# A long convolution with its spectra kept on the chip: three blocks of 192 channels, data as the stationary operand

## The chip, the core and the metric

The kernel runs on one core of a Trainium2 chip. The core has a matrix engine (TensorE; PE in the profile, its weight loads PEld), a vector engine (VectorE, DVE), an activation engine (ScalarE, ACT), a general engine (GpSimd, POOL) and a queue engine (SyncE, SP) that issues nearly all DMA transfers. The engines run side by side, each strictly in the order of its own instructions, and wait for one another by semaphores. Matmuls read the on-chip memory SBUF and write the accumulators in PSUM; ACT or DVE must copy ("evacuate") what stands there back to SBUF.

The metric is the device time of one execution, in microseconds; lower is better. The profiled execution has a span from the first instruction to the last. The engines' busy times and the waits are those of this one execution.

## The reference: what is computed

Two independent parts with 2048 positions and 576 channels each, concatenated. Part A is attention in which each position looks at 8 positions, 2 apart; part B multiplies a long causal convolution (2048 taps for each channel) with q.

```python
def _A_ref(x, wqkv, wo):                 # H = 32 heads of 18, W, dil = 8, 2
    qkv = (x @ wqkv).reshape(B, S, 3, H, Dh).transpose(2, 0, 3, 1, 4)
    q, k, v = qkv[0], qkv[1], qkv[2]
    idx = pos[:, None] - (jnp.arange(W) * dil)[None, :]
    ...
    logits = jnp.einsum("bhsd,bhswd->bhsw", q, kg) * scale
    attn = softmax(where(mask, logits, -1e9))
    o = jnp.einsum("bhsw,bhswd->bhsd", attn, vg)
    return o.transpose(0, 2, 1, 3).reshape(B, S, D) @ wo

def _B_ref(q, k, v, shift_k, ssm_k, ssm_D):
    k_shift = sum(k_pad[:, t:t + S, :] * shift_k[:, ks - 1 - t] for t in range(4))
    kv = k_shift * v
    y_f = rfft(pad(kv, S)) * rfft(pad(ssm_k, S))     # length 4096
    y = irfft(y_f)[:, :S].astype(bfloat16)
    return q * (y + kv * ssm_D)

return jnp.concatenate([_A_ref(...), _B_ref(...)], axis=-1)
```

## The kernel before, in words

The work of both parts is cut into small steps. A long string, `ORDER`, lists them one by one; a table, `STEP`, gives the function for each short name, and the program is emitted in exactly this order. So the order in the string is the order on each engine and on the SP queue. A letter behind a step chooses one of two PSUM pools (`a`, `b`; two buffers of two banks each) and the engine of the evacuation (`s` ACT, `v` DVE; mostly ACT by default, in `evac`, L101 and L103).

Part A: x is loaded and transposed by DMA (`xt`, L357); `qk` and `qt` project it to q and k (L362, L390), `v` to v (L369). For each of the 8 offsets `lm` multiplies q with the shifted k on DVE (L478, L482) and `lb` sums over each head's channels by matmuls (L487, L495). `sm` is softmax in two halves of the positions. `pm` multiplies the weights with the shifted v on DVE (L577), `ps` sums over the 8 offsets (L587, 64 x 64 tiles with the identity), `po` multiplies by wo (L599) and stores.

Part B is a long convolution by a two-level Fourier transform: position = 16 a + b, with 128 values of a in the partitions and 16 of b. `cv` makes the short convolution and kv on DVE, in four chunks of four b (L448, L451, L453). `kt` transposes the filter (L466). `sx` and `kp` are the first level for kv and for the filter: a matmul by a 128-point table `T1` (L419), 128 frequencies in the partitions. A second level has to mix the 16 values of b, so its data must stand differently over the partitions. The kernel does that turn through DRAM: each `sx`/`kp` stores its spectrum to the scratch tensors Dx and Dk (L426), `xl`/`kl` load them turned (L536), `xs`/`ks` are the second level (`s2`, L530, table `W2`), for eight groups of frequencies and channels. `gp` multiplies the two spectra on DVE (L552), all four products of real and imaginary parts, `gi` is the inverse second level (L565, tables `IAt`) and stores to the scratch Dy; `yl` loads it turned (L610), `ys` is the inverse first level (L623) and multiplies with q (L627). `ql` loads q. The tables come from iotas, a bitwise wrap on DVE and a sine on ACT (`t2`, `t3`, `tw`, `ia`).

All large buffers lie in ten areas of SBUF; several buffers with lives one after the other share an area.

Of the kernel before, what the change touches and what calls it, by code (L numbers as in the profile page):

```python
# [10 lines left out]
ALU = mybir.AluOpType  # L11
# [7 lines left out]
tj ld wm.11:b tv t2 xt.3.0 xt.3.1 sk:b lwq.0.0 t3 lwt xt.3.3 xt.3.2 tw xt.3.4 lwq.1.1 qk.0.0.3:a t1 t0 lwq.0.1 lk.0  # L19
cv.0.0 cv.0.1 xt.2.4 lv.0 qk.1.1.3:a t4 cv.0.2 xt.2.0 wt:v cv.0.3 xt.2.2 qk.0.1.3:av xt.2.3 cv.0.4 ia:b qt.3:a xt.2.1  # L20
cv.0.5 lk.1 qk.1.1.2:b lkn.0 lkn.1 cv.0.6 lwq.1.0 lkn.3 cv.0.7 qt.2:b cv.1.1 cv.1.0 qk.0.1.2:a lkn.4 cv.1.2 cv.1.3
cv.1.4 sx.0.0:a lkn.2 xt.1.4 xt.1.0 xt.1.1 xt.1.2 sx.1.0:b qk.1.0.3:b xt.1.3 sx.0.1:a sx.0.2:a cv.1.5 kt.5:bs lk.2
qk.1.0.2:b sx.1.1:a kt.0:a sx.1.2:bv cv.1.6 qk.0.1.1:b kp.0.0:a kp.0.1:bv cv.2.1 qt.1:a xt.0.1 lv.1 kp.0.2:b cv.2.0
qk.0.0.1:a kp.5.0:av xt.0.0 kt.1:b kp.5.1:b xt.0.3 kp.5.2:av xt.0.2 cv.1.7 qk.0.0.2:a kp.1.0:bv t5 kp.1.1:b kt.4:a
xt.0.4 cv.2.2 kp.1.2:a kt.3:bs cv.2.3 cv.2.4 sx.2.0:b qk.1.0.1:a cv.2.5 lk.3 cv.2.6 cv.3.1 sx.2.1:b sx.2.2:b sx.3.0:a
lv.2 qk.0.1.0:a sx.3.1:b sx.3.2:b qk.1.1.1:a cv.3.0 kp.3.0:b kp.3.1:a qt.0:b cv.3.2 lv.3 kp.3.2:a cv.3.3 cv.3.4
qk.0.0.0:b cv.3.5 kp.4.0:b kp.4.1:a kp.4.2:a lwv kt.7:bs qk.1.0.0:b cv.2.7 cv.3.6 kt.2:a cv.3.7 kp.7.0:a kp.7.1:b
kp.7.2:b kt.6:as sx.4.0:b qk.1.1.0:a lm.6.2 lm.0.2 lm.0.0 sx.4.1:b sx.4.2:b v.0:a lm.0.1 sx.6.0:b lm.6.1 sx.6.1:b
lb.0:a sx.6.2:b sx.7.0:a lm.6.0 sx.7.1:b v.2:a sx.7.2:b lb.6:a sx.5.0:b lm.1.0 sx.5.1:a lm.1.1 sx.5.2:b lm.7.0 v.3:a
lb.1:a xl.2 vz kp.2.0:a kp.6.0:b kp.2.1:a lm.7.1 v.8:b lm.4.2 v.5:a xl.3 lm.2.0 lb.7:a lm.2.2 kp.6.1:b kp.2.2:b lm.2.1  # L30
kp.6.2:a v.6:a lb.2:b lm.4.0 v.1:a v.7:b lm.4.1 kl.2 lb.4:b vh.0 lm.3.0 lm.3.1 lm.5.0 v.4:a lb.3:a xs.2.0:b xs.2.1:a
kl.3 lm.5.1 ks.2.0:b lb.5:a vh.1 gp.2.0 vh.2 sm.0.0 sm.1.0 ks.3.0:b xl.0 sm.0.1 ks.2.1:b lwo.3 kl.0 xs.3.0:a ql.0
ks.3.1:b gp.2.1 xs.0.0:a sm.0.2 xs.3.1:b gp.3.0 sm.0.3 gi.3.0:av sm.0.4 gp.3.1 ks.0.0:a xl.1 sm.0.5 sm.1.1 ks.0.1:b
sm.0.6 kl.1 xl.5 xs.0.1:a sm.1.2 gi.3.1:b sm.0.7 gp.0.0 sm.0.8 sm.1.3 ks.1.0:b xs.1.0:a gi.0.0:b kl.5 ql.3 sm.0.10
gp.1.0 ks.1.1:a gp.0.1 lwo.0 pm.0.3 gi.2.0:b xs.1.1:a ks.5.0:b xl.6 kl.6 sm.1.4 gi.0.1:a gi.2.1:b pm.0.1 pm.0.0
ps.0.3:a gp.1.1 ps.0.1:a xs.5.0:a xs.5.1:b pm.0.5 xs.6.0:a gp.5.0 pm.0.4 ks.5.1:b kl.4 ps.0.0:a pm.0.8 sm.1.5 ks.6.0:b
gi.1.0:a ps.0.5:b xl.4 gp.5.1 xs.6.1:a xl.7 gi.1.1:b sm.1.6 ks.6.1:a pm.0.2 gi.5.0:b ps.0.8:a kl.7 gi.5.1:b xs.4.0:a
ks.4.0:b ks.4.1:a ps.0.4:b sm.1.7 yl.1 ql.1 gp.6.0 xs.4.1:a gp.6.1 gp.4.0 lwo.2 gi.6.0:b ps.0.2:a gi.4.0:a lwo.1
pm.0.7 gp.4.1 gi.6.1:b pm.0.6 sm.1.8 ys.1.0:as sm.1.10 yl.3 xs.7.0:b gi.4.1:a xs.7.1:b ks.7.0:a ps.0.7:b ql.5 gp.7.0
ps.0.6:b ks.7.1:a pm.1.1 ys.1.1:bs po.0.0.0 po.0.1.0 yl.0 pm.1.8 gp.7.1 ql.7 ps.1.1:a pm.1.0 yl.2 pm.1.6 gi.7.0:b  # L40
gi.7.1:a ps.1.8:b ys.3.0:as ys.3.1:bs ps.1.0:a ps.1.6:a pm.1.5 ql.2 ys.0.0:bs ys.0.1:bs yl.7 po.0.1.1 pm.1.2 pm.1.4
ps.1.5:b ys.2.0:as yl.5 ys.2.1:a ps.1.2:b pm.1.7 pm.1.3 ps.1.4:a yl.6 po.0.0.1 yl.4 ps.1.7:a ys.7.0:b ys.7.1:as
ps.1.3:av ys.5.0:b ys.5.1:a po.1.0.1 ql.6 ql.4 po.1.0.0 po.1.1.0:v ys.6.0:bs ys.6.1:as ys.4.0:as ys.4.1:bs po.1.1.1
# [4 lines left out]
def kernel(  # L48
# [21 lines left out]
    HD = D // 2  # L70
    PS = bass.MemoryType.PSUM
# [11 lines left out]
    dram = ctx.enter_context(tc.tile_pool(name="dram", bufs=1, space=bass.MemoryType.DRAM))  # L83
# [67 lines left out]
    class Ring:  # L151
# [18 lines left out]
    row0 = const.tile([128, 128], BF16, name="row0")  # L170
    T1 = const.tile([128, 2, 128], BF16, name="T1")
    IB = const.tile([128, 2, 128], BF16, name="IB")
    W2 = const.tile([128, 2, 32, 4, 16], BF16, name="W2")
    IAt = const.tile([128, 3, 16, 128], BF16, name="IAt")
    Eh = const.tile([128, HC + 2, H], BF16, name="Eh")
    maskb = const.tile([128, 32], BF16, name="maskb")
    Db = const.tile([128, D], BF16, name="Db")

    r1, r2, r3, r4, r5, r6, r7, r8, r9, r10 = (
        Area(f"area{i}", n) for i, n in enumerate((18560, 16384, 5 * S, 4 * D, 5 * 2 * D, 19 * D, 28 * D, 2 * S, 5 * D + S + 640, 4 * D)))  # L180
    xns = [(r4 if i < 1 else r2).take(4, D) for i in range(4)]
# [494 lines left out]
```

## Time and profile before

| | us |
|---|---|
| runs | 215.08, 218.06, 219.16; median 218.06 |
| span of the profiled execution | 219.4 |
| DMA moved in it | 50.78 MB, of which HBM read 28.83 MB and written 18.87 MB |
| mean granted TensorE clock | 0.953 |

The table of groups shows for each line and operation the number of instructions, their busy time, the mean in ns and the idle time of the engine just before, with what ended it. The page's DMA part, in transfers, size of one and time from issue to landing:

```profile
Dx<-area SPq DMA_DIRECT2D x16, 288.0 KB, 3.2
Dk<-area SPq DMA_DIRECT2D x16, 288.0 KB, 3.6
...
area<-Dk SPq DMA_DIRECT2D x8, 576.0 KB, 5.5
Dy<-area SPq DMA_DIRECT2D x8, 576.0 KB, 4.0
area<-Dy SPq DMA_DIRECT2D x8, 576.0 KB, 6.1
```

### The profile page before, as it was taken

To read this page: it belongs to the slowest core of one execution; us is meant where nothing else is said; L and a number is where in the kernel's file an instruction comes from. 1 tells how busy PE (TensorE), PEld (TensorE's weight loads), DVE (VectorE), ACT (ScalarE), POOL (GpSimd) and SP (SyncE) were. 2 spreads that over 40 slices of the span, in tenths; PEclk is the share of its full clock that TensorE was granted. 3 is DMA by queue.
4 is the path that set the end of the run, shared out by engine and by line. 5 is a ranking of instruction groups with operands and counts; after the bars stand their busy time and mean duration, and the time that the engine had idled before them with its cause. 6 is when DMAs were issued, how large, how long until landed. Compare 5 with 4: busy or idle time off the path is not lost.

```text
span 219.4 us, 6207 instructions
## 1 busy us (share of the span) xinstructions
PE 193.8 (88%) x2663; PEld 120.3 (55%) x2663; DVE 185.4 (85%) x165; ACT 161.4 (74%) x243; POOL 7.4 (3%) x30
## 2 busy tenths in 40 slices
PE   7696899999899999999998588689995999999890
PEld 2133445556345545566754355556663697777670
DVE  7759996699879999999998899999997399998150
ACT  2627649676699979867479999999995959544442
POOL 7500000000000000000000000000000000000000
PEclk9769599999999999999999969999998899999999
DMA  4799994999997873574769939977999946989984
GB/s 94 150 316 281 371 157 96 279 276 175 226 336 236 225 219 110 184 230 141 209 129 243 352 130 305 288 241 258 341 243 194 348 131 170 355 242 323 266 246 140
DMA packets 60187, 50.78 MB, mean 231 GB/s; under 512 B 14624, under 2 KB 54112, under 8 KB 60160
## 3 DMA queue, kind: packets, MB, share of 16 engines
q1 hardware_dynamic: 60110, 50.24, 82.4%
q8 instruction: 20, 0.33, 0.6%
q0 software_dynamic: 48, 0.15, 0.4%
q14 instruction: 7, 0.06, 0.1%
q10 hardware_dynamic: 2, 0.00, 0.0%
HBM read 28.83 MB, written 18.87 MB: 217 GB/s over the span
## 4 chain that ended last, share of the span: by engine, by line
PE 50%; ACT 15%; DMA 12%; DVE 8%; issue 7%; SPq 6%; ACTq 1%; DVEq 0%
ACT area L101 11%; PE psA L362 8%; PE psA L369 7%; PE psB L362 6%; DMA area<-Dy 4%; PE psA L599 4%; SPq L357 4%; DVE area L577 3%; PE psB L419 3%; DMA out_dram<-area 3%; PE psA L419 2%; DMA area<-in_A_wqkv_dram 2%; PE psB L565 2%; PE psB L369 2%; PE psA L495 2%
## 5 line engine op out<-in xcount | busy, mean ns | idle before, releaser
L101 ACT ACTIVATE area<-psA 128x576 bf16<-128x576 f32 (+5 forms) x112 | 79.3, 745 | 35.2 <-PE psB L599 10.1
L101 ACT ACTIVATE area<-psB 128x576 bf16<-128x576 f32 (+6 forms) x118 | 82.1, 743 | 12.4 <-PE psB L362 4.3
L577 DVE TENSOR_TENSOR area<-area,area 128x4096 bf16<-128x4096 bf16 x18 | 40.6, 2283 | 0.0
L478 DVE TENSOR_TENSOR area<-area 128x4096 bf16<-128x4096 bf16 x16 | 35.6, 2283 | 0.3 <-PE psB L495 0.3
L362 PEld LDWEIGHTS <-area 128*128 128x128 bf16 x160 | 16.5, 104 | 24.6 <-issue 8.2
L362 PE MATMUL psA<-area,area 128*128 128x512 bf16 x100 | 26.0, 411 | 1.9 <-DMA area<-in_A_x_dram 0.9
L448 DVE TENSOR_TENSOR area<-area,area 128x2304 bf16<-128x2304 bf16 x16 | 21.4, 1355 | 5.1 <-DMA area<-in_B_k_dram 4.8
L552 DVE TENSOR_TENSOR area<-area 128x2304 bf16<-128x2304 bf16 x16 | 21.5, 1352 | 4.7 <-ACT area L101 4.7
L530 PEld LDWEIGHTS <-W 128*64 128x64 bf16 x256 | 14.4, 111 | 15.5 <-issue 12.2
L599 PE MATMUL psB<-area,area 32*128 32x288 bf16 x288 | 18.7, 281 | 0.8 <-issue 0.8
L599 PE MATMUL psA<-area,area 32*128 32x288 bf16 x288 | 19.1, 281 | 0.2 <-DVE area L627 0.2
L599 PEld LDWEIGHTS <-area 32*128 32x128 bf16 x576 | 15.9, 93 | 4.0 <-issue 2.7
L587 PEld LDWEIGHTS <-ident 64*64 64x64 bf16 x576 | 15.0, 106 | 5.5 <-issue 3.7
L369 PEld LDWEIGHTS <-area 128*32 128x32 bf16 x360 | 14.1, 141 | 6.5 <-issue 1.3
L369 PE MATMUL psA<-area,area 128*32 128x512 bf16 x280 | 16.6, 382 | 0.5 <-DMA area<-in_A_wqkv_dram 0.5
L565 PEld LDWEIGHTS <-IAt 64*128 64x128 bf16 x256 | 13.1, 99 | 7.0 <-issue 2.7
L530 PE MATMUL psA<-area,W 128*64 128x288 bf16 x136 | 13.1, 292 | 3.9 <-ACT area L101 1.9
L451 DVE TENSOR_TENSOR area<-area,area 128x2304 bf16<-128x2304 bf16 x12 | 16.3, 1354 | 0.2
L362 PE MATMUL psB<-area,area 128*128 128x512 bf16 x60 | 15.3, 405 | 0.0
L530 PE MATMUL psB<-area,W 128*64 128x288 bf16 x120 | 12.8, 310 | 2.0 <-ACT area L101 0.6
L419 PE MATMUL psB<-area,T 128*128 128x384 bf16 x58 | 13.3, 327 | 0.9 <-ACT area L101 0.9
L419 PEld LDWEIGHTS <-T 128*128 128x128 bf16 x96 | 8.8, 98 | 9.7 <-issue 3.7
(107 smaller groups left out, 201.2 us busy)
## 6 DMA issues: line engine op xcount, KB each, us to landing
Dx<-area SPq DMA_DIRECT2D x16, 288.0 KB, 3.2
Dk<-area SPq DMA_DIRECT2D x16, 288.0 KB, 3.6
area<-Dx SPq DMA_DIRECT2D x8, 576.0 KB, 5.1
area<-Dk SPq DMA_DIRECT2D x8, 576.0 KB, 5.5
Dy<-area SPq DMA_DIRECT2D x8, 576.0 KB, 4.0
area<-Dy SPq DMA_DIRECT2D x8, 576.0 KB, 6.1
area<-in_A_wo_dram SPq DMA_DIRECT2D x4, 648.0 KB, 11.5
area<-in_B_k_dram SPq DMA_DIRECT2D x4, 576.0 KB, 5.0
```

The source lines that it names most:

```text
L101: nc.scalar.activation(dst, src, ACT.Copy, **({} if scale is None else {"scale": scale}))
L362: nc.tensor.matmul(ps[:, u, :], w[:, kb, cols[u]:cols[u] + 128], xT[:, kb, t], start=(kb == 0), stop=(kb == 4))
L369: nc.tensor.matmul(ps[32 * a:32 * a + 32, u, :], wv[:, kb, 2 * n + u:D:DH], xT[:, kb, 512 * a:512 * a + 512], start=(kb == 0), stop=(kb == ...
L419: nc.tensor.matmul(ps[:, ri, 0:384], T1[:, ri, :], sf[:, 384 * ch:384 * ch + 384], start=True, stop=not extra)
L448: nc.vector.tensor_tensor(tB if k else tAr[c], kfull[:, 4 * c + 3 - j:4 * c + 7 - j, :], skb[:, j, :].unsqueeze(1).to_broadcast([128, 4, D ...
L451: nc.vector.tensor_tensor(tAr[c], tAr[c], tB, ALU.add)
L478: nc.vector.tensor_tensor(prr.get((n, h)), q2[h], k2[h][:, :, o0:o0 + S], ALU.mult)
L530: nc.tensor.matmul(ps[64 * hp:64 * hp + 64, im, 0:HD], W2[:, im, 8 * g + 2 * prl + hp].rearrange("p l f -> p (l f)"), Wt[:, 2 * prl + hp, ...
L552: nc.vector.tensor_tensor(Pv, Xv.unsqueeze(2).to_broadcast([128, 2, 2, 2 * HD]), Kv.unsqueeze(1).to_broadcast([128, 2, 2, 2 * HD]), ALU.mult)
L565: nc.tensor.matmul(ps[:, hp, 0:HD], IAt[r, tab, 4 * g + 2 * hv + u, :], Pp[(i, hv)][r, n, u, :], start=(n == 0), stop=(n == 3), tile_posit ...
L577: nc.vector.tensor_tensor(Pr.get((hv, p)), vv, Lt[:, :, 256 * hv:256 * hv + 256].unsqueeze(2).to_broadcast([128, W, 2, 256]), ALU.mult)
L599: nc.tensor.matmul(pss[e][:, b, 0:HD], Os[hv][g, d // 2, r, 128 * (d % 2):128 * (d % 2) + 128], wo4[g, d, d0:d1], start=(d == 0), stop=(d ...
```

## The change

The three scratch tensors go, and with them `xl`, `kl`, `yl` and every store into them. The channels are taken in three blocks of 192 (`BD`), each in 48 groups of four channels (`G`).

The first level now holds the data as the stationary operand and streams the table: for each group, a weight of 128 positions a x 64 columns (16 b, 4 channels) and the 128 columns of `T1`, once for the real part and once for the imaginary part, side by side in the two column halves of the array (`first`; steps `sx`, `kp`). The result has (part, b, channel) in the partitions, so that the second level can follow at once: for each of the 128 frequencies one matmul with a table of its own (`E2`) over the 96 columns of kv's and the filter's groups (`second`, steps `s2`). Its result `XKS` holds the spectra of kv and of the filter; `sw` puts a copy of the filter's with its two halves of 64 partitions exchanged beside them by two DMA transfers, `gp` makes two products for each frequency in place (three instructions a block), `gi` is the inverse second level with the products as the stationary operand and the table `F2` as the moving one, and `ys` the inverse first level with one table for each b (`T2`). There is one buffer each for the first level (`A`), the spectra (`XKS`) and the inverse (`B`, over the first third of `XKS`). The D term is added to the filter's tap 0 on POOL (`add_D`) and no longer by a matmul.

The convolution runs over 16 b x 192 channels at a time (3072 elements a partition). The tables: `t3` on POOL, `tc` wrap and sine, `tw` four scalings into `E2`, `tf` for `F2`, `ty` eight steps for `T2`, `tp` small helpers.

Part A changes where the memory map does: x is transposed by DMA twice, quarter by quarter for q and k (`xt`) and again for v (`xv`); the products' buffers for `lm` lie over wq, the last quarters of x and the convolution's buffers; `ps` works in 32 x 32 tiles on four pairs of channels at a time, so that five groups of 128 rows of the attention output come out, and `po` multiplies them as whole arrays, with wo loaded in that arrangement. `ORDER` is rewritten throughout.

```diff
-    dram = ctx.enter_context(tc.tile_pool(name="dram", bufs=1, space=bass.MemoryType.DRAM))
-    Dk = dram.tile([2, 32, 128, HD], BF16, name="Dk")
-    Dx = dram.tile([2, 32, 128, HD], BF16, name="Dx")
-    Dy = dram.tile([2, 32, 128, HD], BF16, name="Dy")
...
+    rA, rX, rQ, rC, rD, rL, rY = (Area(f"area{i}", n) for i, n in enumerate((12288, 18432, 18528, 14464, 13120, 4096, 3072)))
+    A = rA.take(128, 2, G)
...
+    XKS = rX.take(3, G, 128)
+    rX.reset()
+    B = rX.take(2, NT, BD)
...
+    wq = rC.take(5, 2 * D)
+    xqs[1] = rC.take(5, 512)
+    tA, tB = rC.take(NT, BD), rC.take(NT, BD)
+    xqs[0] = xqs[1]
+    rC.reset()
+    prr = Ring(*[rC.take(2, S) for _ in range(3)])
+    phr = Ring(rC.take(2, 2, 512))
...
+    kfs += [rD.take(NT + 3, BD)] * 2
+    kvs += [rD.take(NT, BD)] * 2
...
+    def add_D(q):
+        kn = knr[q]
+        nc.gpsimd.tensor_tensor(kn[0:96, 0:1], kn[0:96, 0:1], Dc[0:96, q:q + 1], ALU.add)
...
+    def t_second():
+        nc.gpsimd.iota(g2, pattern=[[4, 128], [512, 16]], base=0, channel_multiplier=0)
+        nc.gpsimd.tensor_scalar(n2[:, :, 0, :], g2, sc_f[:, 5:6], sc_f[:, 6:7], op0=ALU.mult, op1=ALU.add)
+        nc.gpsimd.tensor_scalar(n2[:, :, 1, :], n2[:, :, 0, :], 2048.0, None, op0=ALU.add)
+
+    def t_wrap(k):
+        r = slice(64 * k, 64 * k + 64)
+        nc.vector.tensor_single_scalar(n2[:, r], n2[:, r], 8191, ALU.bitwise_and)
+        nc.scalar.activation(C2[:, r], n2[:, r], ACT.Sin, bias=pib[:], scale=-2.0 * np.pi / 8192)
+
+    def t_e2(k):
+        nc.vector.tensor_scalar(E2[:].rearrange("p f (r d g) -> p (f r) d g", r=2, d=4)[:, :, k, :],
+                                C2.rearrange("p f r g -> p (f r) g"), dm_e[:, k:k + 1], None, op0=ALU.mult)
...
+    def t_t2(k):
+        nc.gpsimd.iota(tb, pattern=[[1, 2], [16, 128]], base=2 * k, channel_multiplier=0)
+        for ri in range(2):
+            nc.gpsimd.tensor_scalar(tn[:, :, ri, :], tb, sc_f[:, 10:11], 2048.0 * (1 + ri), op0=ALU.mult, op1=ALU.add)
+        nc.vector.tensor_single_scalar(tn, tn, 8191, ALU.bitwise_and)
+        nc.scalar.activation(T2[:, 2 * k:2 * k + 2], tn, ACT.Sin, bias=pib[:], scale=-2.0 * np.pi / 8192)
...
+            nc.vector.tensor_tensor(kvo[e].rearrange("p g b d -> p b g d"), tA.rearrange("p b (g d) -> p b g d", d=4),
+                                    kvs[e].rearrange("p b (g d) -> p b g d", d=4), ALU.mult)
...
+    def first(src, key, e, j):
+        ps = psb()
+        for g in range(8):
+            lhs = src[:, 8 * j + g].rearrange("p b d -> p (b d)")
+            for ri in range(2):
+                nc.tensor.matmul(ps[64 * ri:64 * ri + 64, g // 4, 128 * (g % 4):128 * (g % 4) + 128], lhs, T1[:, ri, :],
+                                 start=True, stop=True, tile_position=(0, 64 * ri))
+        evac(A[:, :, key, 8 * j:8 * j + 8], ps[:].rearrange("p a (g f) -> p f (a g)", g=4))
+
+    def second(e, j):
+        ps = psb()
+        for u in range(8):
+            f = 8 * j + u
+            nc.tensor.matmul(ps[:, u // 4, 128 * (u % 4):128 * (u % 4) + 2 * G], E2[:, f, :], A[:, f].rearrange("p k g -> p (k g)"),
+                             start=True, stop=True)
+        evac(XKS[:, 0:2, :, 8 * j:8 * j + 8].rearrange("p k g f -> p (k g) f"),
+             ps[:].rearrange("p a (u n) -> p n (a u)", u=4)[:, 0:2 * G, :])
+
+    def swap_k(e, r):
+        o = 64 * r
+        nc.sync.dma_start(XKS[o:o + 64, 2], XKS[64 - o:128 - o, 1])
+
+    def g_prod(e, c):
+        g = slice(16 * c, 16 * c + 16)
+        P = XKS[:, 1:3, g, :].rearrange("p t g f -> p t (g f)")
+        nc.vector.tensor_tensor(P, P, XKS[:, 0, g, :].rearrange("p g f -> p (g f)").unsqueeze(1).to_broadcast([128, 2, 2048]), ALU.mult)
+
+    def g_inv(e, j):
+        ps = psb()
+        for g in range(8):
+            for t in range(2):
+                nc.tensor.matmul(ps[:, g // 4, 128 * (g % 4):128 * (g % 4) + 128], XKS[:, 1 + t, 8 * j + g, :], F2[:, t, :],
+                                 start=(t == 0), stop=(t == 1))
+        evac(B.rearrange("p r b (g d) -> p (r b) g d", d=4)[:, :, 8 * j:8 * j + 8, :],
+             ps[:].rearrange("p a (g r d) -> p r (a g) d", g=4, d=4))
...
+        for v in range(4):
+            for ri in range(2):
+                nc.tensor.matmul(ps[:, v // 2, BD * (v % 2):BD * (v % 2) + BD], T2[:, 4 * j + v, ri, :], B[:, ri, 4 * j + v, :],
+                                 start=(ri == 0), stop=(ri == 1))
...
+        for n in range(W):
+            for c in range(m):
+                P = Pr[(hv, 4 * g + c)] if g < 2 else Pr[(hv, 8)]
+                for a in range(4):
+                    r = slice(32 * a, 32 * a + 32)
+                    nc.tensor.matmul(pss[a // 2][32 * c:32 * c + 32, a % 2, 0:w], ident[r, r],
...
+        for di, (d0, d1) in enumerate(DCH):
+            for g in range(5):
+                nc.tensor.matmul(ps[:, di, 0:HD], Os[hv][:, g, a, 128 * u:128 * u + 128], wo5[:, g, d0:d1],
+                                 start=(g == 0), stop=(g == 4))
```

The part of the new order from the second level of block 0 to the first `lm`, and the end of the order:

```
s2.0.12:bv s2.0.8:a cv.1.6 kt.1.1:bs qk.0.1.1:b qk.1.1.1:a qt.1:a lk.2 cv.1.7 sx.1.5:b kp.1.5:b sx.1.1:a sw.0.0 sw.0.1
qk.0.0.1:a cv.2.0 lv.2 cv.2.1 kp.1.3:b t5 cv.2.2 lkn.5 sx.1.2:b kp.1.0:a qk.1.0.1:a xt.0.2 sx.1.0:b kp.1.4:b gp.0.1
xt.0.4 sx.1.4:a gp.0.0 gp.0.2 gi.0.3:a xt.0.1 gi.0.0:bv gi.0.1:b gi.0.4:av cv.2.3 gi.0.5:a cv.2.4 gi.0.2:b sx.1.3:a
cv.2.5 xt.0.0 cv.2.6 xt.0.3 cv.2.7 kp.1.1:b xv.0.2 qt.0:a qk.1.1.0:bv qk.0.0.0:a lm.0.2 qk.1.0.0:a ql.0 qk.0.1.0:b
...
po.0.2.1:a pm.1.5 pm.1.4 pm.1.6 pm.1.8 po.0.1.1:b po.0.3.1:b ys.2.2:a ys.2.1:a ps.1.1:b ps.1.2:av po.1.1.0:b
po.1.2.0:bv po.1.3.0:av po.1.3.1:b po.1.1.1:bv po.1.2.1:av po.1.0.0:av po.1.0.1:a
```

495 lines of the change are left out of this document (205 added, 290 removed).

## The prediction, made before the changed kernel was run

> **What bounds the kernel now.** I read the busy times of the profile page first, then the busy time of each engine by stage, then the instructions by form, then the chain of waits and the list of who waits for whom.
>
> ```profile
> span 219.4 us, 6207 instructions
> ...
> PE 193.8 (88%) x2663; PEld 120.3 (55%) x2663; DVE 185.4 (85%) x165; ACT 161.4 (74%) x243; POOL 7.4 (3%) x30
> ```
>
> PE has the largest number, but its matmuls overlap and their ends are modelled, so I look at which engine has no holes. The stages below are cut where DVE's work changes: tables, the convolution by the short kernel (`cv`), the products q·k (`lm`), softmax, the products with v (`pm`) and the end.
>
> ```profile
> 0.00:15.60 15.60, 12.48 (x35) 4.16 (x36) 9.98 (x28) 6.38 (x8) 7.11 (x29) 0.78 0.75 187
> 15.60:74.30 58.70, 53.85 (x330) 29.35 (x328) 51.20 (x45) 44.49 (x58) 0.00 (x0) 0.94 0.96 240
> 74.30:114.90 40.60, 39.77 (x589) 23.86 (x589) 40.02 (x21) 30.94 (x42) 0.33 (x1) 1.00 0.64 181
> 114.90:135.60 20.70, 16.06 (x180) 9.60 (x175) 18.86 (x23) 20.54 (x35) 0.00 (x0) 0.92 0.80 253
> 135.60:200.00 64.40, 58.02 (x1193) 42.86 (x1192) 59.05 (x42) 52.53 (x93) 0.00 (x0) 0.97 0.88 260
> 200.00:219.40 19.40, 13.62 (x345) 10.45 (x344) 6.32 (x11) 6.50 (x11) 0.00 (x0) 1.00 0.81 231
> ```
>
> After the length, the columns are PE, PEld, DVE, ACT, POOL (with instruction counts), the granted clock, the DMA share and GB/s. DVE's holes are 5.6, 7.5, 0.6, 1.8, 5.4 and 13.1 us, 34.0 in all: almost none between the first convolution and the last product, the rest at both ends. So time = DVE's work + DVE's holes = 185.4 + 34.0. ACT is level with DVE in the softmax stage alone. DMA stands at 0.96 in the second stage and holds DVE up there only now and then:
>
> ```profile
> DVE area L448 <- DMA area<-in_B_k_dram: 4.8, 2, 2.5
> DVE area L552 <- ACT area L101: 4.7, 3, 3.3
> ```
>
> That is the point of the argument: the DRAM scratch that the change removes costs DMA time, and DMA is not what DVE waits for, except in these 4.8 us (a first load of k, which stays) and part of the 4.7 us (late spectra).
>
> **DVE's work, part by part.** These are the prices:
>
> ```profile
> L577 DVE TENSOR_TENSOR area<-area,area 128x4096 bf16<-128x4096 bf16 x18 | 40.6, 2283 | 0.0
> ...
> L448 DVE TENSOR_TENSOR area<-area,area 128x2304 bf16<-128x2304 bf16 x16 | 21.4, 1355 | 5.1 <-DMA area<-in_B_k_dram 4.8
> ...
> L103 DVE CAST area<-psB 128x768 bf16<-128x768 f32 x3 | 2.9, 954 | 0.6 <-PE psB L419 0.5
> ...
> L326 DVE TENSOR_SCALAR area<-area 128x1024 int32<-128x1024 int32 x1 | 1.0, 1046 | 0.0
> ...
> L103 DVE COPY area<-area 128x640 bf16<-128x640 bf16 x1 | 0.3, 321 | 0.0
> ```
>
> The first two rows give 0.52 ns an element and 0.16 us an instruction for a two-tensor operation. The q·k products, the v products and softmax are untouched. The convolution keeps its elements (32 x 2304 = 24 x 3072) and loses 8 instructions: -1.3 us. Its last multiply now writes runs of four elements; I keep the price, since pairs stay together, and put up to +6 us (3 x 3072 elements at the 954/768 ns of the cast) in the range. The spectrum products keep theirs too (16 x 2304 = 9 x 4096): -1.1. The final products with q (16 x 576 = 12 x 768): -0.6. DVE's evacuations go from 15 to 18 by the letters in the two orders, about the cast's 0.95 us each: +2.9.
>
> The tables grow. A table for every one of 128 frequencies (`t3`, `tc`, `tw`) replaces one for 32 pairs:
>
> ```profile
> 5.20:7.20 2.00, 1.70 (x13) 1.00 1.04 239
> 7.20:12.80 5.60, 4.43 (x6) 0.57 0.78 186
> ```
>
> These two stretches, for DVE alone, hold the old `t3` and `tw`: 6.1 us go; the first, with 13 tiny instructions in 1.70 us, prices those at 0.13 us. New are two wraps of 2048 int32 at twice the 1.05 us row (4.1), eight wraps of 512 for the last table (8 x 0.52 = 4.2), some 21 tiny instructions of `tp` and `tf` (2.7 and 0.3 for a small product), and four scalings of 4096 bf16 in `tw`. The last have no row. From below they go like the copy of 640 (0.321 us, hence about 1.3 us), from above like the int32 row (4.2 us). I take 1.3 us, as the copy shares their types: 5.1 in all, with +11.6 kept for the range.  Tables: 16.4 - 6.1 = +10.3.
>
> DVE's work is then 185.4 - 1.3 - 1.1 - 0.6 + 2.9 + 10.3 = 195.6 us, at most 195.6 + 6 + 11.6 = 213. Nothing reaches much below 195.6, as every price sits at the cheapest row.
>
> **The holes, stage by stage.** Start: the index table now comes from POOL, which must do an iota and two scalings of 2048 int32.
>
> ```profile
> L311 POOL IOTA area<- 128x512 int32 x1 | 0.6, 647 | 0.0
> ```
>
> At four times that row each, some 7.8 us from about 3 us on, while DVE has 8 us of small tables before the first wrap: a hole of about 3 us, where the wait for k was. I keep 5.6; scalings at twice the price add 5. `add_D` is new on POOL and waits for the filter's load, with only later table steps queued behind it.
>
> Second stage: k and v come in three blocks, and blocks 1 and 2 share one buffer, so the wait for k stays. New is the exchange of the halves of the filter's spectrum (`sw`) ahead of `gp`. It moves 64 x 12,288 B = 786 KB, twice.
>
> ```profile
> area<-Dx SPq DMA_DIRECT2D x8, 576.0 KB, 5.1
> ...
> area<-area SPq DMA_DIRECT2D x3, 18.0 KB, 2.1
> ```
>
> From these rows 786 KB take 2.1 + 3.0 x 786/576 = 6.2 us. DVE has three convolution steps (3 x 1.75 us) in between for block 0, more for block 1: with the two halves side by side about 1 us shows, one after the other 7. At the stage's 240 GB/s the 1.57 MB of both take 6.6 us, so I take 1. SBUF — State Buffer in the Trainium skill (Door 1: The DMA port swizzle) says that a tile of 64 partitions reaches only 8 of 16 ports and measured 196 GB/s. By it one exchange takes about 4 us (an estimate), and nothing would show; no row of this trace is such an exchange.
>
> On SP's queue the five loads `xt.0` (the last quarter of x) stand behind the waiting `sw.0`, and behind them the last `qk` steps and so every `lm`:
>
> ```profile
> 0.81 1.22 SPq L357
> ...
> 47.12 0.62 PE psB L466 x10
> ...
> 48.39 2.17 PE psA L362 x10
> ```
>
> Five issues (6.1 us) and four `qk` steps and a half (9.8 us) make 16 us; five convolution steps and the products of block 0 (8.8 + 6.9) give DVE as much to do. With a little over for the landing I take 9 for 7.5; were that cover gone, 16 us would show.
>
> Third stage: `lm` now shares its time with the spectra of blocks 1 and 2.
>
> ```profile
> L101 ACT ACTIVATE area<-psB 128x768 bf16<-128x768 f32 x26 | 20.6, 819 | 3.4 <-DMA Dx<-area 1.8 <-PE psA L362 1.3 <-PE psB L419 0.3
> L101 ACT ACTIVATE area<-psA 128x1024 bf16<-128x1024 f32 x16 | 16.4, 1023 | 13.6 <-PE psA L362 7.6 <-PE psA L369 6.0
> ```
>
> Between the first `lm` and the last `lb` the order gives ACT 35 evacuations of 768, 21 of 1024 and 8 others: 28.7 + 21.5 + about 6 = 56 us, against 40.0 + 6.9 + 4.8 + 2.6 = 54 us of DVE. Two engines level with each other in fixed orders wait for one another: 4 us for 0.6. Softmax stays at 1.8. In the `pm` stage the reload of the inverse's scratch goes: 2.5 for 5.4. At the end eight `po` steps of ten whole-array matmuls replace four of 72 quarter-array ones with as many streamed columns; from the last `pm` I expect 17 us for 19.4, of which DVE has 5: 12 for 13.1. Holes: 5.6 + 9 + 4 + 1.8 + 2.5 + 12 = 34.9.
>
> Sum: 195.6 + 34.9 = 230.5, say 231 us, on the scale of the profiled 219.4; the median of the three runs is 218.06, inside the same scatter (215.08 to 219.16), so I make no correction.
>
> **PE.** Streamed columns of whole-array passes hardly change: `sx` and `kp` 96 x 384 = 576 x 128 / 2, `second` 256 x 288 / 2 = 384 x 96, `gi` 256 x 288 / 2 = 288 x 128. What changes is the weights loaded for so few columns.
>
> ```profile
> 149.39 1.00 PE psB L587 x32
> 150.39 0.61 PE psA L530 x8
> 151.00 1.08 PE psB L565 x16
> ```
>
> Ten transposes, each with a fresh 128 x 128 weight and 128 columns, took 0.62 us above (the row of L466), 62 ns each. `second` and the inverse at that price cost 23.8 and 17.9 us against 256 x 0.61/8 = 19.5 and 256 x 1.08/16 = 17.3. `first` (576) costs between 31 ns each, if its two column halves overlap as the 64 x 64 tiles of L587 do, and 62: 18 to 36 us. I take 18, from that row.
>
> **Rivals.** *DMA was the pacer after all* (faster). Scratch traffic gone, the loads land early and the holes shrink to those that no order can fill: 4 us at the start, 12 at the end, 2 between. 195.6 + 18 = 213.6, say 213. It decides when DVE's holes fall under 18; for it speaks the 0.96 of DMA in the second stage, against it that DVE's holes put down to DMA are 5 us.
>
> *The tables are paid from the holes* (no change): holes of 24, from an earlier `pm` stage and a start filled with table work: 219.5.
>
> *The exchange is the new wait* (slower): one buffer each for spectra, products and inverse makes second, exchange, product, inverse, output and the next second one chain. With the halves one after the other (2 x 6.2 us) and 5.3 us of cover, blocks 0 and 2 show 7 each: 231 + 14 = 245. For it speaks DMA's share of 0.8 and more in four stages, against it the order, which puts more of DVE's work between for block 1.
>
> *PE's small matmuls* (slower): `first` at 62 ns adds 18 us, three quarters of it before `lm` may begin, as its buffers lie on those of x, wq and the convolution: 231 + 13 = 244. For it speaks PE's 53.85 of 58.70 us in the second stage, against it the 31 ns of L587's tiles. TensorE: Matmul & The Clock Gate in the Trainium skill (Back-to-back issue gap) gives about 81 ns for each weight load and matmul of 128 columns in a stream. By it `second`, the inverse and `first` with its halves overlapping would take some 18 us more (an estimate), this rival's price; the trace's 62 ns speaks against it.
>
> That the change doesn't do what it says is not a rival: no scratch is left to go through.
>
> **Numbers.** Forecast 0.54; DMA the pacer 0.07; paid from the holes 0.18; exchange 0.10; small matmuls 0.11. The forecast's own range is 223 to 241. The range of 8 in 10 leaves out the DMA case and the worst ends (213 + 35 = 248): 217 to 248. Two per cent, 4.4 us, is about what a measurement of this kernel can tell from no change. Faster is the DMA case, 0.07; within 2% (213.7 to 222.4) the second rival and the forecast's lowest edge, 0.20; slower the rest, 0.73.
>
> **What would show it.** DVE busy 194 to 200 us if the prices hold; `tw` above 2 us each or the convolution's last step above 2.5 would break them. `lm` should begin near 90 us, not 74; ACT should be full from there to softmax; the last `pm` should end some 17 us before the span's end. A DVE wait for a transfer from area to area above 5 us would prove the exchange; PE without holes up to `lm`, with `first` near 62 ns, the small matmuls. A DVE with holes under 20 us would prove the forecast wrong.

## The result, and the profile after

The changed kernel takes 230.21 us (median of four runs, 228.85 to 231.58) against 217.50 us (215.08 to 219.16) for the kernel before: a ratio of 1.0625, 95% interval 1.0547 to 1.0703. It is slower by 12.7 us by these medians. Times of the kernel before scatter, so the ratios leave out its runs that lie more than 1.5% above the fastest one beside them (here 219.16), and its profiled execution was itself a long one, with a span above the whole time of each of its measured runs. The spans of the two profiled executions therefore lie only 8.6 us apart (228.0 and 219.4).

The page of the changed kernel, busy time of each engine, then DMA and the shares of the chain that ended last:

```profile
span 228.0 us, 6663 instructions
...
PE 184.6 (81%) x2963; PEld 130.7 (57%) x2963; DVE 203.3 (89%) x164; ACT 159.3 (70%) x193; POOL 48.4 (21%) x66
...
DMA packets 57555, 27.71 MB, mean 122 GB/s; under 512 B 51445, under 2 KB 56309, under 8 KB 57142
...
PE 27%; DVE 24%; POOL 15%; ACT 10%; DMA 10%; issue 8%; SPq 4%; DVEq 0%; POOLq 0%; ACTq 0%
```

The scratch traffic is gone (27.71 MB for 50.78), PE is 9 us lighter, and yet the time is longer, as DVE is 17.9 us busier. POOL, at 48.4 us for 7.4, holds 15% of the chain. The same six stages as before the change, again with columns length, PE, PEld, DVE, ACT, POOL, granted clock, DMA share and GB/s:

```profile
0.00:20.28 20.28, 6.73 (x16) 2.36 (x17) 17.09 (x34) 7.05 (x9) 17.35 (x25) 1.00 0.82 169
20.28:93.79 73.51, 67.66 (x831) 43.78 (x830) 65.49 (x48) 62.53 (x75) 28.32 (x38) 0.98 0.70 147
93.79:149.62 55.83, 46.65 (x829) 35.72 (x828) 53.36 (x36) 49.41 (x65) 0.61 (x2) 0.97 0.67 124
149.62:164.04 14.42, 12.07 (x213) 10.69 (x210) 12.91 (x18) 11.50 (x11) 1.56 (x2) 1.00 0.81 174
164.04:212.36 48.32, 40.36 (x937) 29.70 (x937) 48.32 (x25) 25.02 (x31) 0.57 (x1) 0.96 0.19 50
212.36:228.00 15.64, 11.15 (x144) 8.45 (x144) 6.09 (x10) 3.79 (x5) 0.00 (x0) 0.95 0.32 102
```

By stage the difference is +4.7 us before the first convolution step, +14.8 from there to the first `lm`, +15.2 from `lm` to softmax, then -6.3, -16.1 and -3.8. So work has moved forward (the second level, the products and the inverse now lie ahead of softmax), and the whole is 8.6 us longer. DVE's holes, length less busy time, are 3.2, 8.0, 2.5, 1.5, 0.0 and 9.55: 24.7 us for 34.0 before. DVE's work grew by 17.9 us, its holes shrank by 9.3.

DVE's groups that bear on this (count, then busy us and mean ns, then idle time before):

```profile
L511 DVE TENSOR_TENSOR area<-area 128x4096 bf16<-128x4096 bf16 x9 | 20.1, 2288 | 3.8 <-DMA area<-area 3.8
...
L366 DVE TENSOR_SCALAR E<-area 128x4096 bf16<-128x4096 bf16 x4 | 5.4, 1366 | 0.0
L374 DVE TENSOR_SCALAR area<-area 128x16 int32<-128x16 int32 x1 | 5.4, 5373 | 0.0
L471 DVE TENSOR_TENSOR area<-area,area 128x3072 bf16<-128x3072 bf16 x3 | 5.3, 1755 | 0.1
...
L386 DVE TENSOR_SCALAR area<-area 128x512 int32<-128x512 int32 x8 | 4.1, 514 | 5.3 <-POOL area L385 5.3
...
L362 DVE TENSOR_SCALAR area<-area 128x2048 int32<-128x2048 int32 x2 | 3.3, 1674 | 0.0
```

The four scalings of `tw` (L366), the last step of the convolution (L471) and the wraps (L386, L362) cost about what was forecast. One row does not fit at all: L374, on sixteen int32 numbers a partition, lasts longer than two products of 4096. DVE's timeline around it, and below it POOL's in the same time (start, length, instruction):

```profile
5.81 1.97 DVE L370 TENSOR_SCALAR area<-area 128x4 bf16<-128x4 int32 x1
7.68 0.28 DVE L373 TENSOR_SCALAR area<-area 128x16 int32<-128x16 int32 x1
7.88 5.37 DVE L374 TENSOR_SCALAR area<-area 128x16 int32<-128x16 int32 x1
...
14.89 1.15 DVE L362 TENSOR_SCALAR area<-area 128x2048 int32<-128x2048 int32 x1
...
18.16 2.20 DVE L362 TENSOR_SCALAR area<-area 128x2048 int32<-128x2048 int32 x1
20.28 1.74 DVE L466 TENSOR_TENSOR area<-area,area 128x3072 bf16<-128x3072 bf16 x1
...
32.95 1.92 DVE L466 TENSOR_TENSOR area<-area,area 128x3072 bf16<-128x3072 bf16 x1
```

```profile
5.70 2.06 POOL L357 TENSOR_SCALAR area<-area,area 128x2048 int32<-128x2048 int32 x1 [1.63 <-DVE area L350]
7.84 5.38 POOL L358 TENSOR_SCALAR area<-area 128x2048 int32<-128x2048 int32 x1
...
18.22 1.05 POOL L261 MEMSET area<- 64x1152 bf16 x1
...
32.18 3.03 POOL L385 TENSOR_SCALAR area<-area,area 128x256 int32<-128x256 int32 x2 [1.21 <-ACT T L387]
```

L370 ends with POOL's L357, L374 with POOL's L358; the second L362 is 1.05 us longer than the first, the length of the POOL memset beside it. The reader sees a wait that no semaphore shows: the profile counts it as DVE's busy time.

### The profile page after: what moved, and what is told of

It reads as the page before. It is cut to its first block, busy times and chain, and to the rows that moved or that the text cites. A ratio compares the mean times of both kernels' runs of the same rounds, so it can differ in the third digit from the quotient of the medians.

```text
span 228.0 us, 6663 instructions
## 1 busy us (share of the span) xinstructions
PE 184.6 (81%) x2963; PEld 130.7 (57%) x2963; DVE 203.3 (89%) x164; ACT 159.3 (70%) x193; POOL 48.4 (21%) x66
## 2 busy tenths in 40 slices
DMA packets 57555, 27.71 MB, mean 122 GB/s; under 512 B 51445, under 2 KB 56309, under 8 KB 57142
## 4 chain that ended last, share of the span: by engine, by line
PE 27%; DVE 24%; POOL 15%; ACT 10%; DMA 10%; issue 8%; SPq 4%; DVEq 0%; POOLq 0%; ACTq 0%
DVE area L596 10%; ACT area L103 9%; DMA area<-area 8%; POOL area L385 7%; PE psA L422 7%; DVE area L511 5%; SPq L415 4%; POOL area L358 2%; PE psA L623 2%; PE psB L623 2%; DVE area L545 2%; PE psA L439 2%; PE psB L422 2%; PE psB L439 2%; DMA area<-in_A_x_dram 2%
## 5 line engine op out<-in xcount | busy, mean ns | idle before, releaser
L103 ACT ACTIVATE area<-psA 128x1024 bf16<-128x1024 f32 (+7 forms) x95 | 81.0, 885 | 26.7 <-PE psA L422 6.8
L103 ACT ACTIVATE area<-psB 128x1024 bf16<-128x1024 f32 (+4 forms) x81 | 73.9, 949 | 23.4 <-PE psB L607 6.9
L545 DVE TENSOR_TENSOR area<-area 128x4096 bf16<-128x4096 bf16 x16 | 35.8, 2287 | 0.3 <-PE psB L439 0.3
L439 PEld LDWEIGHTS <-area 128*128 128x128 bf16 x160 | 15.3, 98 | 18.0 <-issue 0.4
L511 DVE TENSOR_TENSOR area<-area 128x4096 bf16<-128x4096 bf16 x9 | 20.1, 2288 | 3.8 <-DMA area<-area 3.8
L491 PEld LDWEIGHTS <-area 128*64 128x64 bf16 x576 | 17.2, 111 | 11.0 <-issue 8.2
L499 PEld LDWEIGHTS <-E 128*128 128x128 bf16 x384 | 18.6, 100 | 8.4 <-issue 7.9
L385 POOL TENSOR_SCALAR area<-area,area 128x256 int32<-128x256 int32 x16 | 19.6, 1228 | 5.6 <-ACT T L387 4.7
L623 PEld LDWEIGHTS <-area 128*128 128x128 bf16 x160 | 15.3, 98 | 6.4 <-issue 1.1
L422 PE MATMUL psA<-area 128*32 128x512 bf16 x280 | 16.9, 381 | 2.5 <-issue 1.9
L517 PEld LDWEIGHTS <-area 128*128 128x128 bf16 x288 | 16.3, 98 | 4.0 <-issue 2.9
L469 DVE TENSOR_TENSOR area<-area 128x3072 bf16<-128x3072 bf16 x9 | 15.9, 1771 | 0.2
L491 PE MATMUL psB<-T,area 128*64 128x128 bf16 x336 | 12.8, 225 | 4.0 <-ACT area L103 2.4
L499 PE MATMUL psA<-area,E 128*128 128x96 bf16 x208 | 13.2, 211 | 1.9 <-ACT area L103 1.4
L466 DVE TENSOR_TENSOR area<-area 128x3072 bf16<-128x3072 bf16 x8 | 14.1, 1778 | 0.1
```

What stands on the lines that cost most here:

```text
L103: nc.scalar.activation(dst, src, ACT.Copy, **({} if scale is None else {"scale": scale}))
L385: nc.gpsimd.tensor_scalar(tn[:, :, ri, :], tb, sc_f[:, 10:11], 2048.0 * (1 + ri), op0=ALU.mult, op1=ALU.add)
L422: nc.tensor.matmul(ps[32 * a:32 * a + 32, u, :], wv[:, kb, 2 * n + u:D:DH], xT[:, kb, 512 * a:512 * a + 512], start=(kb == 0), stop=(kb == ...
L439: nc.tensor.matmul(ps[:, u, :], wq[:, kb, c:c + 128], xqs[j][:, kb], start=(kb == 0), stop=(kb == 4))
L469: nc.vector.tensor_tensor(tA, tA, tB, ALU.add)
L491: nc.tensor.matmul(ps[64 * ri:64 * ri + 64, g // 4, 128 * (g % 4):128 * (g % 4) + 128], lhs, T1[:, ri, :], start=True, stop=True, tile_pos ...
```

## The experiments

The first theory behind the runs: DVE's list is the bound, and the new index tables, with POOL's part in them, are what it pays. Rivals: the exchange, DVE's evacuations as a cost that another engine could take, PE's small matmuls, and, on the kernel before, DMA as its pacer. The runs of before beside them had medians of 218.43 us (`e1` to `e4`), 218.46 (`b1`, `b2`, `e5`, `e7`) and 216.07 (`e8`, `e9`). For the second group no ratio is given, as the runs of before beside it spread from 214.20 to 221.32. Differences from the changed kernel are taken from its 230.21 us above, which comes from another group of runs; as the medians of before move by 2.4 us from group to group, differences of that size are not resolved.

**e1: the second scaling of the index table on DVE.**

```diff
 def t_second():
-        nc.gpsimd.tensor_scalar(n2[:, :, 1, :], n2[:, :, 0, :], 2048.0, None, op0=ALU.add)
 def t_wrap(k):
+        nc.vector.tensor_scalar(n2[:, r, 1, :], n2[:, r, 0, :], 2048.0, None, op0=ALU.add)
```

> The second scaling of the 2048 indices (+2048) leaves POOL and becomes two instructions of 1024 on DVE. Theory A (DVE's list sets the time, and DVE instructions are held while POOL works): POOL loses its instruction of 5.4 us, the 16-element instruction on DVE that took 5.37 us falls below 0.3 us, the first convolution step starts near 16 us instead of 20.3, DVE busy near 198 us, time 226 us (224 to 228) for 230.2. Theory B (the chain spectrum, exchange, product, inverse with PE and ACT sets the time): the start is not on the path, 229 to 231 us.

Measured: 225.99 us, ratio 1.0372 (1.0319 to 1.0424): 4.2 us less than the changed kernel. DVE's timeline in this run:

```profile
7.89 0.31 DVE L374 TENSOR_SCALAR area<-area 128x16 int32<-128x16 int32 x1
...
16.40 1.74 DVE L466 TENSOR_TENSOR area<-area,area 128x3072 bf16<-128x3072 bf16 x1
```

The sixteen elements take 0.31 us for 5.37, and the first convolution step starts 3.9 us earlier. DVE has two more instructions and is 3.2 us less busy (200.1).

**e2: no index work for the two large tables.** The scalings on POOL and the wraps on DVE go; the sines read the bare iotas.

```diff
-        nc.gpsimd.tensor_scalar(n2[:, :, 0, :], g2, sc_f[:, 5:6], sc_f[:, 6:7], op0=ALU.mult, op1=ALU.add)
-        nc.gpsimd.tensor_scalar(n2[:, :, 1, :], n2[:, :, 0, :], 2048.0, None, op0=ALU.add)
...
-        nc.vector.tensor_single_scalar(n2[:, r], n2[:, r], 8191, ALU.bitwise_and)
...
-        for ri in range(2):
-            nc.gpsimd.tensor_scalar(tn[:, :, ri, :], tb, sc_f[:, 10:11], 2048.0 * (1 + ri), op0=ALU.mult, op1=ALU.add)
-        nc.vector.tensor_single_scalar(tn, tn, 8191, ALU.bitwise_and)
```

> Leaves out the scalings on POOL and the wraps on DVE for the second-level table and the table T2; the sines run on the bare iotas, so the tables' contents are wrong. Everything else stands. Theory A: DVE loses some 7.5 us of wraps, about 10 us in which POOL holds it and 5 us of waits for POOL; DVE busy near 187 us, time 214 us (211 to 218), the time of the kernel before. Theory B: 224 us or more.

Measured: 220.18 us, ratio 1.0106 (1.0047 to 1.0164), between the two theories. The index work is worth 10.0 us of the 12.7 (by the ratios 5.2 of 6.25 per cent). DVE is busy 189.4 us, 13.9 less; the wraps that went are only 7.4 of these, so the other 6.5 were for the most part DVE held by POOL. Not all of it comes out in the time, since other things are late next; the page of this run, then two of its waits:

```profile
PE 184.2 (84%) x2954; PEld 130.8 (60%) x2963; DVE 189.4 (87%) x154; ACT 158.7 (73%) x193; POOL 19.9 (9%) x48
...
DVE area L465 <- DMA area<-in_B_v_dram: 4.2, 1, 4.2
...
DVE area L460 <- DMA area<-in_B_k_dram: 2.8, 2, 1.8
```

A kernel that starts its convolution at 10.7 us instead of 20.28 waits for k and v there.

**e3: no exchange.**

```diff
-        nc.sync.dma_start(XKS[o:o + 64, 2], XKS[64 - o:128 - o, 1])
+        pass
...
+        nc.gpsimd.memset(rX.t[:, 17400:18432], 0.0)
```

> Leaves out the exchange of the halves of the filter's spectrum (six transfers of 768 KB); the second product uses what stands in the buffer. Theory A: only the 3.8 us that DVE waits for these transfers can go, and the loads queued behind them come earlier: 227 us (225 to 229). Theory B: the exchange is the link of the chain, 218 us or less.

Measured: 228.47 us, ratio 1.0481 (1.0408 to 1.0554): 1.7 us less than the changed kernel by the times and about 3 by the ratios, inside theory A's range. The exchange as the new wait falls. Yet the page of the changed kernel counts 8% of its span, some 18 us, on these transfers in the chain that ended last. Both are true: without these transfers the chain that ends last runs over PE and the loads of x instead, and is nearly as long.

**e4: eleven DVE evacuations to ACT.** The letter `v` is taken from nine steps of the order up to softmax, and the two `kt` steps without an `s` get one; the first of each:

```diff
-s2.0.1:av
+s2.0.1:a
...
-kt.1.0:b
+kt.1.0:bs
```

> Eleven evacuations (five of second, two of the inverse, one of qk, one of lb, two of the transposed filter) move from DVE to ACT, in the same places of the order. Theory A: DVE loses 11 us, ACT (159 us busy) takes 10 more: DVE busy near 192 us, time 222 us (219 to 226). Theory B: ACT is a link of the chain and the time rises, 231 to 236 us.

Measured: 236.62 us, ratio 1.0848 (1.0782 to 1.0913). Theory A fell: DVE has 10.3 us less to do (193.0), and the kernel is 6.4 us slower, as theory B had it (a little above its range). Its waits:

```profile
DVE area L511 <- DMA area<-area: 9.5, 2, 8.0
DVE area L545 <- PE psB L439: 5.8, 1, 5.8
```

Two things in SP's queue come later; first the changed kernel, then this run (L506 is the exchange, L410 the loads of `xt.0`):

```profile
64.24 3.46 SPq L506 DMA_DIRECT2D area<-area  x2
...
76.57 7.47 SPq L410 DMA_TRANSPOSE area<-in_A_x_dram  x5
```

```profile
67.78 1.18 SPq L506 DMA_DIRECT2D area<-area  x2
...
79.81 8.51 SPq L410 DMA_TRANSPOSE area<-in_A_x_dram  x5
```

ACT alone evacuates block 0's second level later, and all that follows on PE is 3.2 us late: the last `qk` step on the quarter of x loaded before (`xt.1`), the loads `xt.0` of the last quarter, and the `qk` steps on it. So the first `lm` of 4096 elements (L545) waits 5.8 us for PE and begins at 100.14 us, for 95.31. The exchange, issued 3.5 us later, makes DVE wait 8.0 us before its products, but it does not hold the loads `xt.0`, though they stand behind it in the queue. By the code these two quarters of x share one buffer, and the queue waits for PE; first its wait in the changed kernel, then the loads in e3, which has no exchange:

```profile
SPq L410 <- PE psB L491: 4.0, 1, 4.0
```

```profile
76.45 7.74 SPq L411 DMA_TRANSPOSE area<-in_A_x_dram  x5
```

Without the exchange they start at 76.45 us, for 76.57. DVE's list is thus not the only bound: the chain second level, evacuation, the steps behind it on PE, x, `qk` is level with it up to `lm`.

**e5: all scalings of the tables on DVE** (e1, and those of `t_t2` too).

```diff
-            nc.gpsimd.tensor_scalar(tn[:, :, ri, :], tb, sc_f[:, 10:11], 2048.0 * (1 + ri), op0=ALU.mult, op1=ALU.add)
+            nc.vector.tensor_scalar(tn[:, :, ri, :], tb, sc_f[:, 10:11], 2048.0 * (1 + ri), op0=ALU.mult, op1=ALU.add)
```

> The changed kernel with the second scaling of 2048 indices and the sixteen scalings of 256 for T2 on DVE; POOL keeps the iotas and the first scaling. DVE gets 16 x 0.3 = 4.8 us of work more, loses 5.3 us of waits for POOL and most of the time in which POOL holds it. Theory A: DVE busy near 200 us as in the run with the second scaling alone, 224 us (222 to 226) against its 226.0. Theory B (moving work to DVE costs what it is long): 230 us.

Measured: 224.37 us (224.32 to 224.71), 5.8 less than the changed kernel: theory A's time, though not its 200 us for DVE. The page:

```profile
PE 184.6 (83%) x2954; PEld 130.6 (59%) x2963; DVE 203.3 (91%) x182; ACT 159.2 (71%) x193; POOL 23.8 (11%) x49
```

The 203.3 us of DVE are the same to the digit, with 18 more instructions in them: what was held time is now work, and the waits for POOL's L385 (5.3 us) are gone. This is the fastest version that keeps the whole computation, and it stays slower than the kernel before.

**e7: each matmul of the second level twice.**

```diff
         for u in range(8):
             f = 8 * j + u
+            for _ in range(2):
...
```

> The changed kernel with each of the 384 matmuls of the second level issued twice (same result): 384 x 62 ns = 24 us more for PE, nothing for any other engine. Theory A (PE has slack except in the second level of block 0, where ACT's evacuations at 0.69 us a tile already set the pace): 233 us (230 to 237). Theory B (PE's small matmuls set the time): 248 us or more.

Measured: 236.57 us (236.43 to 236.93), 6.4 more for 384 more weight loads and matmuls, 17 ns each. That is inside theory A's range; theory B, PE's small matmuls as the bound, falls. They do not come for nothing, though: the first `lm` of 4096 elements begins at 98.6 us for 95.3, so half of the 6.4 us is lost before it.

**e8: the small table F2 behind the wraps.**

```diff
-tp tf tv sk:a
+tp tv sk:a
...
-kt.0.1:as tc.1 xt.2.1
+kt.0.1:as tc.1 tf xt.2.1
```

> The seven small DVE instructions of the table F2 are moved behind the two wraps of the second level's index table; nothing else changes, so DVE has nothing in flight while POOL does its second scaling of 2048. In the changed kernel that scaling took 5.38 us, and the 16-element DVE instruction beside it 5.37. Theory A (POOL's scaling costs what it costs, and holds DVE's scalar instructions until it is done): the scaling lasts 5.4 us again with DVE waiting for it, the seven instructions take 0.2 to 0.3 us each in their new place, and the first convolution step begins at about 21 us, for 20.28: 231 us (229.5 to 232.5). Theory B (the two engines hold each other; alone the scaling goes at the 2.06 us of the first one): the first wrap begins about 3 us sooner and the first convolution step before 18 us: 227 us (225 to 229).

Measured: 232.64 us, ratio 1.0816 (1.0722 to 1.0911). POOL's timeline, then DVE's:

```profile
5.60 2.06 POOL L357 TENSOR_SCALAR area<-area,area 128x2048 int32<-128x2048 int32 x1 [1.70 <-DVE area L350]
7.75 5.38 POOL L358 TENSOR_SCALAR area<-area 128x2048 int32<-128x2048 int32 x1
...
15.22 1.02 POOL L385 TENSOR_SCALAR area<-area,area 128x256 int32<-128x256 int32 x2
```

```profile
13.16 1.23 DVE L362 TENSOR_SCALAR area<-area 128x2048 int32<-128x2048 int32 x1 [6.75 <-POOL area L358]
...
20.20 0.29 DVE L374 TENSOR_SCALAR area<-area 128x16 int32<-128x16 int32 x1
...
25.34 0.43 DVE L379 TENSOR_TENSOR F<-area 128x256 bf16<-128x256 bf16 x1 [3.90 <-ACT area L378]
```

With DVE idle beside it, L358 again takes 5.38 us: that is POOL's own price, and it was DVE that was held. That is theory A; its 21 us for the first convolution step (25.68) and the upper end of its range (232.5) were missed, because F2's sine on ACT now comes late and DVE waits 3.90 us for it. The page of this run:

```profile
PE 185.1 (80%) x2963; PEld 131.3 (57%) x2963; DVE 197.2 (86%) x164; ACT 159.3 (69%) x193; POOL 44.8 (19%) x66
```

DVE has the same 164 instructions in another order and is 6.1 us less busy: about that much of its 203.3 us was waiting, and the 6.5 us from e2 agree.

**e9: neither the index work nor the exchange** (the edits of e2 and e3 together).

> Both without the index work of the two large tables (their sines read the bare iotas) and without the exchange of the filter's halves (a region that is cleared once stands for it). Theory A (the two costs add up, as neither is behind the other): 220.2 - 1.7 = 218.5 us (217 to 220), level with the kernel before. Theory B (with the index work gone DVE waits for the exchange and for what stands behind it on SP's queue, so that its removal now brings more): 213 to 216 us, faster than before.

Measured: 219.04 us, ratio 1.0170 (1.0107 to 1.0233): theory A. Against the runs of before beside it, this is no better than e2's 1.0106; the exchange costs between nothing and 3 us by the two pairs of runs. What is late are the loads of v and k:

```profile
DVE area L466 <- DMA area<-in_B_v_dram: 5.0, 1, 5.0
...
DVE area L461 <- DMA area<-in_B_k_dram: 2.7, 2, 1.7
```

**b1: the kernel before with a quarter of its scratch loads** (32 of 128 partitions of each).

```diff
-        nc.sync.dma_start(Wr.get((key, i)), by_rt(Dd, i // 4, i % 4))
+        nc.sync.dma_start(Wr.get((key, i))[0:32], by_rt(Dd, i // 4, i % 4)[0:32])
...
-            nc.sync.dma_start(Wr.get(("y", i)), by_f1(Dy, dh, 8 * c4, 8))
+            nc.sync.dma_start(Wr.get(("y", i))[0:32], by_f1(Dy, dh, 8 * c4, 8)[0:32])
```

> The kernel before, with 24 loads from the three DRAM scratch tensors reading 32 of 128 partitions (the other partitions keep what stood there, so part B of the output is wrong); stores, steps and order stand. 10.4 MB of 50.8 go. Theory A (the scratch hardly sets the time): only the waits for late spectra, 3 to 5 us, can shrink: 216 us (213 to 218) for 218.4. Theory B (DMA is the pacer of the kernel before): 209 us or less.

Measured: 213.96 us (213.32 to 216.61), with 40.18 MB moved for 50.78. That is 4.5 us below the median of the runs of before beside it (218.46), but only 0.2 below the lowest of them (214.20). Theory B, with 209 us or less, falls as far as these loads go; the stores stood. Whether the loads cost anything is not shown by the times. In the profile the wait of the products for late spectra (L552) is 2.9 us, for 4.7.

**b2: the kernel before with eight convolution multiplies twice** (10.8 us more work for DVE, no other change).

```diff
+            for _ in range(2 if k in (1, 3) else 1):
             nc.vector.tensor_tensor(tB if k else tAr[c], kfull[:, 4 * c + 3 - j:4 * c + 7 - j, :],
...
```

> The kernel before, with eight of the convolution's sixteen multiplies issued twice (same result): 8 x 1.355 = 10.8 us more for DVE in the second stage, nothing for any other engine. Theory A (DVE's list sets the time of the kernel before): 228 us (225 to 230) for 218.4. Theory B (the holes of DVE's list swallow it): 221 us or less.

Measured: 224.41 us (222.34 to 224.67), just below theory A's range. That is 6.0 us above the median of the runs of before beside it, but 10.2 above the lowest of them, for 10.8 us of work (10.4 by DVE's busy time, 195.8 us for 185.4). So DVE's list does set the time for the greater part, and how much of the added work went into its holes is not shown. In the profiles the holes are 27.2 us for 34.0, but the granted clock of the first 30 us differs as well (0.94 here, 0.77 in the profile of before), and one of the holes that went was a wait for PE.

## Why the prediction was right, and where its steps were not

The forecast was 231 us for 230.21, and its sum stood on the scale of the profiled executions: 230.5 against 228.0 measured. The direction was right, and so was the table work as the main cause: e2 shows 10.0 of the 12.7 us there. But of the three parts of that cost the prediction had only one, the wraps on DVE (7.4 us). DVE held by POOL (some 6.5 us) and DVE's waits for POOL's L385 (5.3 us) were not in it. The two terms of the sum were off by 8 and 10 us, in opposite ways; that the total came out so near is luck.

**DVE's work: 195.6 forecast, 203.3 measured.** By its own sign, "DVE busy 194 to 200 us if the prices hold", not all of them held. Most rows came as priced: `tw` 1.37 us each for 1.3, the convolution's last step 1.755 for 1.75 (its upper end of +6 us was not needed), the wraps 7.4 for 8.3, the products 20.1 us, 1.4 less than before, for -1.1. The evacuations and the int32 copies from PSUM together went from 12.6 to 16.0 us by their groups, +3.4 for +2.9. The step that failed is "some 21 tiny instructions of `tp` and `tf` (2.7 and 0.3 for a small product)". The rows that priced them came from a stretch without such POOL work beside it; here two of them ran beside POOL's scalings and ended with those (L370 after 1.97 us, L374 after 5.37). The Trainium skill has a rule for it, on the page SBUF — State Buffer (Who interferes with whom): a VectorE instruction in a two-port mode, or with two inputs in SBUF beside a GpSimd instruction that reads SBUF, needs a pair of ports that it shares with GpSimd; whichever comes first has the pair for its whole instruction, and the other waits in full. The trace agrees (L374: 5.37 us beside 5.38), but no row shows in which mode L374 ran. The prediction priced POOL and DVE as if they were independent, and cited another section of that page.

**The holes: 34.9 forecast, 24.7 measured.** The stages came out at 3.2, 8.0, 2.5, 1.5, 0.0 and 9.55 us for 5.6, 9, 4, 1.8, 2.5 and 12. The prediction kept most of them near their value in the kernel before, as if a longer list of DVE's left the holes alone. It also called them "almost none between the first convolution and the last product", where its own figures (7.5, 0.6, 1.8 and 5.4) make 15.3 of the 34.0. The holes are other ones now. DVE's wait for k, "which stays" in the prediction (4.8 us), shows no more, nor does its wait for late spectra (4.7 us); two of the largest are new, as the rows of L386 and L511 above show: 5.3 us for POOL's L385 and 3.8 us for the exchange.

So the second stage's 8.0 us for 9 is a near hit by chance: more than half of it (4.3) is the wait for POOL's L385, which was not forecast. Of 17.9 us more DVE work 12.7 appear in the time; that added work by itself fills holes was to be shown by b2, and is not. The rival "tables are paid from the holes" put the holes at 24, as measured, but on top of the 195.6 us of DVE work.

**Start.** POOL's iota and two scalings were forecast at 2.6 us each; they took 2.24, 2.06 and 5.38. The 3 us hole did not show as one: DVE was held, which the profile counts as busy. The first convolution step began at 20.28 us, for 15.60 before.

**The exchange.** 8.5 us each by the page, for 6.2:

```profile
area<-area SPq DMA_DIRECT2D x6, 768.0 KB, 8.5
```

The cover was larger than forecast, too: DVE waited for it 3.8 us in three waits, 2.4 at the longest. The estimate of about 4 us by the Trainium skill's page (SBUF — State Buffer, Door 1: The DMA port swizzle) was for one transfer alone. Here the two of a block overlap and each lasts about twice that, so no run here shows it.

**`lm` and ACT.** The first `lm` was forecast near 90 us and began at 93.79; most of the lateness is the start's (in e1 it began at 90.11). The prediction had the loads `xt.0` held by the exchange ahead of them in SP's queue. That step was wrong: e3 shows that they wait for PE. PE's order up to the last `qk` steps is what stands level with DVE's list here, as e4 shows; in the changed kernel DVE waits only 0.3 us for it. ACT was to be full from `lm` to softmax; it is busy 49.41 of 55.83 us, and the strided evacuations kept about their price, 845 ns for 819 at 768 elements, and 1051 for 1023 at 1024:

```profile
L103 ACT ACTIVATE area<-psA 128x1024 bf16<-128x1024 f32 x44 | 45.1, 1051 | 17.2 <-PE psA L422 6.8 <-PE psA L607 4.7 <-PE psA L439 4.6
```

**The end.** 15.6 us from the last `pm`, for 17.

**PE.** From the chain of waits of the changed kernel, `gi` (L517) and `first` (L491), 16 matmuls each:

```profile
82.63 1.05 PE psA L517 x16
...
84.58 0.57 PE psA L491 x16
```

That is 66 ns for 62, and 36 ns for `first`, near the 31 that was taken: its column halves overlap. The rival of the small matmuls falls with this and with e7. The 81 ns of the Trainium skill's page (TensorE: Matmul & The Clock Gate, Back-to-back issue gap) is above what this trace shows.

**Where the expected gain went.** The change removes 23 MB of transfers. By b1, with 10.6 MB less, the kernel before is between 0.2 and 4.5 us faster, so what the scratch was worth is not shown. Whatever comes of it is in the 9.3 us by which the holes shrank; the index work took it back and more. What is left of the difference in e9 (1.7%, interval 1.1 to 2.3) was not taken apart; its DVE waits 5.0 us for v and 2.7 for k.

## What to carry to other kernels

When work is moved to an idle engine, ask what it shares with the engine that sets the time: one scaling of 5.38 us on POOL held DVE for its whole length, and moving the scalings to DVE was 5.8 us faster. An instruction whose duration does not go with its size may be waiting; look at what ends at the same moment on the neighbour. A transfer in the chain that ended last is not worth its length: the exchange had 8% of that chain, and its removal gave 1.7 us. And a sum "work + holes" needs both terms forecast anew: here 17.9 us more work went with 9.3 us fewer holes in the profiles, and the holes that were left had other causes.

## What the runs showed of the hardware that was not expected

In these traces DVE and POOL hold each other, in both directions. DVE's instruction on 16 int32 elements took 5.37 us beside POOL's scaling and 0.31 us without (e1). POOL's pair of scalings of 256 elements (L385) took 1.02 us with DVE idle (e8, at 15.22) and 3.03 us beside DVE's convolution (at 32.18), where DVE's own multiply took 1.92 us for 1.74. No wait is shown for either; the time is counted as busy.

POOL's two scalings of 2048 int32 elements differ: 2.06 us from a contiguous source, 5.38 us (2.6 ns an element) for the one whose source and destination are both runs of 16 out of 32; e8 shows that DVE is not the cause. Whether it is the layout, or the form without scalars from memory, was not tried.
